# A fused attention and MLP kernel: P V of the fourth batch as float32r products in parts, a rank for attention units, and the order of the tails' transfers

## The chip, the cores and the metric

One NeuronCore of a Trainium2 chip runs the whole program. The metric is device time in microseconds (us) of one execution; lower is better. The engines are named as the profile names them: PE is TensorE (PEld its weight loads), DVE is VectorE, ACT is ScalarE, POOL is GpSimd, SP the engine on whose queue most transfers are issued.

## The reference

Attention with rotary embedding over 4 batches, 8 heads, 576 positions and 64 columns a head; then two MLPs over the 512 columns of x, all in float32:

```
attn = softmax(rot(q) rot(k)^T / sqrt(64)) v          # 4 x 8 x 576 x 64
x  = attn, heads side by side                          # 4 x 576 x 512
xn = (x - mean) / sqrt(var + 1e-6) * g_ln
x  = x + relu(xn w_ch1) w_ch2                          # 512 -> 2048 -> 512
h  = gelu(x w_in);  u, v = halves of h                 # 512 -> 2 x 512
v  = (v - mean) / sqrt(var + 1e-6) * g2_ln
v  = w_sg v + b_sg                                     # over positions, 576 x 576
out = x + (u * v) w_out
```

## The kernel before

Activations lie transposed: columns on the partitions, positions along the free axis, in halves of HQ = 288. A large product is made of three float32r passes: both operands are split into a rounded high part and the rest, and high x high, low x high and high x low are summed in PSUM. The rounding is a copy on ACT, the rest a subtraction on DVE.

**Attention** (class Attn) runs in 64 units: four batches (groups 0 to 3), each eight blocks (a head pair p and a half hi), each block two heads j. A unit (`unit`, lines 302 to 366) does ten passes of scores (line 311: five key chunks, K and X each holding high and low part), a maximum over chunks (DVE, 334), a maximum over partitions (POOL, 337), then either adds the negative maximum on PE (`add`, 392) and takes the exponential (395), or subtracts it on DVE into sT (`subtract`, 376) and takes it there (381). The second form runs once all first-MLP weights are converted, so in most of batches three and four. Then P V (line 350): five products, one per key chunk, with sT and v as plain float32. The trace shows each as two passes, 640 in 64 units. Two ACT copies (357, 360) move the result and the row sums; the sums go by a transfer (364) to where the normalisation reads them. S is one tile, so a unit's scores wait until the one before has been subtracted; sT has two buffers (SB), K has four (KB).

**The first MLP** works on a batch at a time: `ln` and `rest` centre and split x (477 to 563; 512 the centred x, 524 and 528 its high and low part), `up` (655 to 657, relu parts 663 and 665) and `down` (685 to 687, ends 699 or 702, and in the last pass 708, 710 and the store 713). It runs on PE between the attention's steps of a later batch. Weights come in double precision and are converted while batch one and two are at work (lines 47 to 55, 635, 637). x0 has 17 tiles, so attention runs two batches ahead at most: two units of batch four run at 431 and 438 us, the other fourteen from 498 us on.

**The order** of all engines up to the end of the first MLP is written by a planner in the kernel, `Sched`: each step is a generator's yield of (engine, earliest start, cost, rank). It takes the step that can start first; a step of lower rank on the same engine that could start within HOLD = 0.4 of the chosen step's cost goes ahead of it. Ranks: relu and down ends 1, `ln` and `rest` 2, k, q and v preparation 3 to 3.2, weight loads 3.5, conversions 4, the second MLP's first loads 4.5, MLP products 5. A unit has rank 0 up to P V, which has 0.5. Engines keep that order on the chip.

**The second MLP** (`moe2`) begins as such a task when the last `up` pass has finished its first half (line 775 counts): `load_x(0)` issues eight transfers of x (937) and splits its four column slices on ACT (949) and DVE (951), the last two of them after `through()`, the end of the last up product. Then `load_tails(0)` issues four transfers (977) of the last 64 positions of batches one and two and splits them (ACT 981, DVE 983). The rest of `moe2` is ordered by the compiler's scheduler behind and between the planned steps: v in five chunks of positions (1006 to 1008, the fifth from the tails), each with its gelu (919 to 922) and statistics (1012, 1013), u (1038 to 1040), the root (1014, 1015), the normalisation and split of v (1019, 1023, 1025), the product over positions (1054 to 1058), and the output (963 to 967).

Of the kernel before, what the change touches and what calls it, by code (L numbers as in the profile page):

```python
# [14 lines left out]

NC5 = 5
HQ = 288
SB, QB, KB, AB = 2, 3, 4, 1
WB, WX, CB = 8, 3, 4
KC = (0, 256, 576)  # L20
KEY0 = (0, 128, 256, 384, 448)
L_CONV = 10.0
HOLD = 0.4
FG = [4, 8, 8, 4]

AHEAD = 2
# [6 lines left out]
def f32(ap):  # L33
    return ap.bitcast(F32)
# [90 lines left out]
def latest(*xs):  # L125

    return None if any(x is None for x in xs) else max(xs)


class Attn:  # L130
# [10 lines left out]
    def __init__(self, tc, ctx, k, groups, sched):  # L141
        self.tc, self.nc, self.k, self.groups, self.c = tc, tc.nc, k, groups, sched
        self.p = ctx.enter_context(tc.tile_pool(name="attn", bufs=2, side="right"))
        self.ps = ctx.enter_context(tc.tile_pool(name="attn_ps", bufs=1, space=PS))
        self.S = self.ps.tile([128, NC5, 512], F32, tag="S", name="S")
        self.Sfree = [0.0, 0.0]
        self.PV, self.X, self.qin, self.kin, self.vfree, self.sT = Bank(), Bank(2), Bank(QB), Bank(2), Bank(2), Bank(SB)
        self.K = Bank(KB)
        self.vin = [self.p.tile([128, NC5, 192], F32, tag=f"vin{i}", name=f"vin{i}", bufs=1) for i in range(2)]
        self.sums = [self.p.tile([64, HQ], F32, tag=f"sums{i}", name=f"sums{i}", bufs=1) for i in range(3)]  # L150
        self.last = {}
        self.done = []
        self.blocks, self.units = [], []
        for g, (b, halves) in enumerate(groups):
            if g == 0:
                order = [(hi, p) for hi in range(2) for p in range(4)]
            else:
                order = [(hi, p) for p in range(4) for hi in range(2)]
            for n, (hi, p) in enumerate(order):
                B = dict(g=g, b=b, hi=hi, h=halves[hi], p=p, n=len(self.blocks), left=2, k0=None, k=None, q=[None, None], v=None)  # L160
                self.blocks.append(B)
                B["newk"] = hi == 0
                B["newv"] = g == 0 or hi == 0
# [39 lines left out]
        return e  # L203

    def new_K(self, B):
        B["kslot"] = self.K.take()
        B["K"] = [self.p.tile([128, 576], F32R, tag=f"K{j}", name=f"K{j}", bufs=KB) for j in range(2)]

    def first(self):

# [36 lines left out]
    def prep(self, bi):  # L247

        nc, c, B = self.nc, self.c, self.blocks[bi]

        def k_task():
            e = yield "SP", self.kin.free, 0.7
            slot = self.kin.take()
            kin = self.p.tile([128, 2, 576], F32, tag="kin", name="kin")
            nc.sync.dma_start(out=kin, in_=self.k["k"][B["b"], B["p"]])
            yield "DVE", lambda: latest(e + 7.5, self.K.free()), 0.0
            self.new_K(B)
            e = yield from self.turn_k(kin, B["K"], 0, 576, 0.0)
            B["k0"] = B["k"] = e + 0.1
            self.kin.give(slot, e)  # L260

        def q_task():
            e = yield "SP", self.qin.free, 0.6
            slot = self.qin.take()
            qin = self.p.tile([128, 2, HQ], F32R, tag="qin", name="qin", bufs=QB)
            nc.sync.dma_start(out=f32(qin), in_=self.k["q"][B["b"], B["p"]][:, :, HQ * B["h"]:HQ * B["h"] + HQ])
            e = yield from self.rope(f32(qin), HQ, HQ * B["h"], e + (5.0 if bi == 1 else 7.0))
            e = yield from self.split(f32(qin[:, 0, :]), qin, e)
# [12 lines left out]

        if B["newk"]:
            c.task(k_task(), 3)
        c.task(q_task(), 3.1)

    def load_v(self, bi):
        nc, B = self.nc, self.blocks[bi]

        def v_task():
            e = yield "SP", self.vfree.free, 0.7  # L290
            slot = B["vslot"] = self.vfree.take()
            t = B["vin"] = self.vin[slot]
            for j in range(2):
                if j:
                    e = yield "SP", 0.0, 0.7
                nc.sync.dma_start(out=t[:, :, 128 * j:128 * j + 64], in_=self.k["v"][B["b"], B["p"]][:, :, j, :])
            B["v"] = e + 5.5

        if B["newv"]:
            self.c.task(v_task(), 3.2)  # L300


    def unit(self, i):
# [20 lines left out]
        if B["left"] == 0:  # L324
            self.X.give(B["xslot"], e + 0.1)
        Kb["kusers"] -= 1
        if Kb["kusers"] == 0:
            self.K.give(Kb["kslot"], e + 0.1)
        if i + 1 < len(self.units):
            c.task(self.unit(i + 1), 0)  # L330
        self.ahead(i)
        e = yield "DVE", e + 0.35, 1.68
        mx = self.p.tile([128, HQ], F32, tag="mx", name="mx", bufs=1)
# [6 lines left out]
        else:  # L340
            x1, slot, sT = yield from self.add(am, e)
        V = B["vof"]
        ps = None
        for c0, c1 in ((0, 2), (2, 5)):
            e = yield "PE", (lambda: latest(x1, self.PV.free(), V["v"])) if c0 == 0 else 0.0, 0.51 * (c1 - c0), 0.5
            if c0 == 0:
                bank = self.PV.take()
                ps = self.ps.tile([128, 512], F32, tag="PV", name="PV")[:, 0:HQ]
            for ch in range(c0, c1):
                nc.tensor.matmul(ps, V["vin"][:, ch, 64 * j:64 * j + 128], sT[:, ch, :], start=ch == 0, stop=ch == 4)  # L350
        self.sT.give(slot, e)
        V["users"] -= 1
        if V["users"] == 0:
            self.vfree.give(V["vslot"], e)
        a, b = 64 * j, 64 - 64 * j
        yield "ACT", e + 0.35, 0.41
        nc.scalar.copy(self.k["x0"](g, p, hi)[a:a + 64], ps[a:a + 64])  # L357
# [6 lines left out]
        nc.sync.dma_start(out=self.sums[self.sums_of(g, hi)][r:r + 1], in_=t[b:b + 1])  # L364
        if u["ends"]:
            self.done.append(e + 3.0)

    def new_sT(self):
        return self.sT.take(), self.p.tile([128, NC5, HQ], F32, tag="sT", name="sT", bufs=SB)
# [54 lines left out]
def fused_kernel(ctx, tc, q, k, v, cs, cst, w12, wi, wo, wsg, wsg4, gb, out):  # L424
# [35 lines left out]
        return x0_rel.get(x0_order[len(x0_order) - 17])  # L460

    attn_ctx = ExitStack()
    attn = Attn(tc, attn_ctx, dict(q=q, k=k, v=v, cs=csb, e=e128, x0=get_x0, x0_free=x0_free, spare=lambda: stored[0] == 32), groups, C)
    cctx = ExitStack()
    cpool = cctx.enter_context(tc.tile_pool(name="conv", bufs=1, side="right"))

# [285 lines left out]
    def mlp(parts):  # L752
        for d, g, F, i, hh in parts:
            n = FG[g]
            if g not in left:
                yield "PE", lambda: 0.0 if g != 1 or stored[0] == 32 else None, 0.0
                left[g] = 8
                if g == 1:
                    cctx.close()
                open_h(g)  # L760
                if g == NG - 1:
                    last_group()
            steps = down(g, F, i, hh) if d else up(g, n * F + i, hh)
# [135 lines left out]
def moe2(tc, M, hp, wpool, pp, B, x1d, w, gbt, eps, out, through):  # L899
# [23 lines left out]

    X = {}

    def load_x(b):
        if b >= B:
            return
        x1, at = {}, {}
# [9 lines left out]
        for c in range(4):  # L939
            if c == 2:  # L940
                yield "SP", lambda: 0.0 if through() else None, 0.0
            if c % 2 == 0:
                xh.append(M.tile([128, 2, 576], F32R, tag="xh", name="xh", bufs=2))
                xl.append(M.tile([128, 2, 576], F32R, tag="xl", name="xl", bufs=2))
# [27 lines left out]
    def load_tails(b):  # L972

        s = M.tile([128, 512], F32, tag="sq", name="tails", bufs=2)
        for c in range(4):
            e = yield "SP", 0.0, 0.6
            nc.sync.dma_start(out=s[:, 128 * c:128 * c + 128].rearrange("p (b q) -> p b q", b=2),
                              in_=x1d[b:b + 2, c, :, 512:576].rearrange("b p q -> p b q"))
        e = yield "ACT", (e or 0.0) + 4.0, 0.63
        tails[b] = t = M.tile([128, 2, 512], F32R, tag="w", name="w", bufs=WB)  # L980
        nc.scalar.copy(t[:, 0, :], s)
# [1 line left out]
        nc.vector.tensor_tensor(t[:, 1, :], s, f32(t[:, 0, :]), ALU.subtract)  # L983

    def at_once(steps):
        for _ in steps:
            pass

    yield from load_x(0)
    yield from load_tails(0)  # L990
    yield None
    for b in range(B):
        x1, xh, xl = X[b]
# [49 lines left out]
            final(b - 1)  # L1043
        at_once(load_x(b + 1))
        if b % 2 and b + 1 < B:
            at_once(load_tails(b + 1))
        gt = {}
        for hh in range(2):
            qs = slice(HQ * hh, HQ * hh + HQ)
# [79 lines left out]
```

## Time and profile before

| | us |
|---|---|
| median of 3 runs | 999.93 (998.19 to 1001.24) |
| profiled execution | 1002.52 |
| its span on the core | 1000.7 |
| PE busy | 939.7 |
| DVE busy | 714.2 |
| ACT busy | 444.6 |
| POOL busy | 91.4 |

The span runs from the first to the last instruction of the program; the execution's own time has 1.8 us around it. Busy times are of one execution, and engines overlap: 939.7 us of PE leave 61 us of the span in which it did nothing. PE's busy time counts a pass from its issue to its modelled end, so the distance between starts, not the duration, is what a pass costs in a row of passes. A groups row gives how many instructions of one line and shape there were, their busy time, the mean of one, and the idle time before them with what ended it.

### The profile page before, as it was taken

The numbers are of one execution on the slowest core, as the hardware profiler recorded it, in microseconds if no ns is written. First come the engines' busy times: TensorE is split into PE (matmuls) and PEld (weight loads), VectorE is DVE, ScalarE is ACT, GpSimd is POOL, SyncE is SP. The second block draws the span as 40 slices with busy tenths as digits, with TensorE's granted clock in tenths as the row PEclk, the third lists the DMA queues.
The fourth block names the chain that finished last, engine by engine and source line by source line (L and its number), as shares of the span: only waits on it lengthen the run. The fifth ranks groups of instructions, "written<-read, shape, count | busy, mean of one in ns | idle before, by whom it ended". The sixth has DMA issues, their size and how long they took to land.

```text
span 1000.7 us, 15881 instructions
## 1 busy us (share of the span) xinstructions
PE 939.7 (94%) x6057; PEld 867.8 (87%) x6057; DVE 714.2 (71%) x1188; ACT 444.6 (44%) x901; POOL 91.4 (9%) x78
## 2 busy tenths in 40 slices
PE   4688899999998889999999999999999979999998
PEld 3566688798898778989998999999999969989998
DVE  6998666699788788865589744586553887667764
ACT  3564554665434355443235531425222546345441
POOL 1121112122000211100012110000000000000000
PEclk9899999999999899999999999999999989999999
DMA  9888444378464564653755533588763300303011
GB/s 273 240 283 263 110 106 109 104 202 258 152 207 146 189 213 134 204 163 121 251 182 145 156 128 127 192 285 273 250 204 91 90 1 12 95 2 89 1 49 48
DMA packets 93420, 153.76 MB, mean 154 GB/s; under 512 B 38048, under 2 KB 60576, under 8 KB 93344
## 3 DMA queue, kind: packets, MB, share of 16 engines
q1 hardware_dynamic: 92800, 152.16, 49.1%
q8 instruction: 48, 0.79, 0.3%
q10 hardware_dynamic: 544, 0.59, 0.2%
q14 instruction: 28, 0.23, 0.1%
HBM read 107.25 MB, written 26.21 MB: 133 GB/s over the span
## 4 chain that ended last, share of the span: by engine, by line
PE 73%; DVE 14%; DMA 5%; ACT 2%; issue 2%; POOL 2%; SPq 1%; DVEq 0%; ACTq 0%; POOLq 0%
PE PV L350 8%; PE S L311 7%; PE m L686 6%; PE m L685 6%; PE m L687 6%; PE m L655 5%; PE m L657 5%; PE m L656 5%; DVE mx L334 4%; DMA sums<-sr 3%; PE S L392 2%; PE p L1054 2%; PE p L1055 2%; PE p L1056 2%; DVE sT L376 2%
## 5 line engine op out<-in xcount | busy, mean ns | idle before, releaser
L350 PE MATMUL PV<-sT,vin 128*128 128x288 f32 x640 | 170.8, 413 | 3.6 <-ACT sr L360 1.8
L655 PE MATMUL m<-xh,w 128*128 128x288 f32 x480 | 148.0, 308 | 2.4 <-DVE h L665 2.3
L350 PEld LDWEIGHTS PV<-sT,vin 128*128 128x128 f32 x640 | 120.1, 194 | 32.7 <-ACT sr L360 2.7
L685 PE MATMUL m<-h,w 128*128 128x288 f32 x480 | 145.2, 302 | 0.0
L686 PE MATMUL m<-h,w 128*128 128x288 f32 x480 | 142.0, 296 | 0.0
L334 DVE TENSOR_REDUCE mx<-S 128x288 f32<-128x1440 f32 x64 | 106.0, 1657 | 49.9 <-PE S L311 48.8
L656 PE MATMUL m<-xl,w 128*128 128x288 f32 x480 | 141.5, 295 | 0.0
L657 PE MATMUL m<-xh,w 128*128 128x288 f32 x480 | 141.2, 294 | 0.0
L687 PE MATMUL m<-h,w 128*128 128x288 f32 x480 | 140.5, 293 | 0.0
L337 POOL PARTITION_ALL_REDUCE am<-mx x64 | 89.3, 1395 | 500.4 <-DVE mx L334 500.4
L311 PE MATMUL S<-X,K 128*128 128x288 f32 x640 | 112.6, 321 | 16.8 <-ACT X L200 10.2
L311 PEld LDWEIGHTS S<-X,K 128*128 128x128 f32 x640 | 95.5, 201 | 29.2 <-ACT sT L395 11.0
L665 DVE SCALAR_TENSOR_TENSOR h<-m,h 128x288 fp32r<-128x288 f32 x128 | 58.0, 454 | 66.6 <-ACT h L663 65.8
L655 PEld LDWEIGHTS m<-xh,w 128*128 128x128 f32 x480 | 90.0, 188 | 6.5 <-DVE h L665 3.6
L663 ACT ACTIVATE h<-m 128x288 fp32r<-128x288 f32 x128 | 52.2, 408 | 95.0 <-PE m L657 94.5
L656 PEld LDWEIGHTS m<-xl,w 128*128 128x128 f32 x480 | 90.2, 188 | 1.4
L686 PEld LDWEIGHTS m<-h,w 128*128 128x128 f32 x480 | 90.2, 188 | 1.0
L685 PEld LDWEIGHTS m<-h,w 128*128 128x128 f32 x480 | 90.0, 188 | 1.1
L657 PEld LDWEIGHTS m<-xh,w 128*128 128x128 f32 x480 | 90.3, 188 | 0.0
L687 PEld LDWEIGHTS m<-h,w 128*128 128x128 f32 x480 | 90.2, 188 | 0.0
L357 ACT COPY x<-PV 64x288 f32<-64x288 f32 x64 | 25.2, 394 | 137.8 <-PE PV L350 137.7
L395 ACT ACTIVATE sT<-S 128x576 f32<-128x576 f32 x74 | 53.6, 769 | 29.7 <-PE S L392 28.3
(149 smaller groups left out, 1848.9 us busy)
## 6 DMA issues: line engine op xcount, KB each, us to landing
w<-wsc SPq DMA_DIRECT2D x96, 512.0 KB, 4.3
X<-qin SPq DMA_DIRECT2D x124, 144.0 KB, 2.6
cd<-in_w SPq DMA_DIRECT2D x32, 512.0 KB, 6.1
wsc<-w SPq DMA_DIRECT2D x24, 512.0 KB, 3.6
qin<-in_q SPq DMA_DIRECT2D x31, 288.0 KB, 4.4
kin<-in_k SPq DMA_DIRECT2D x15, 576.0 KB, 5.0
vin<-in_v SPq DMA_DIRECT2D x40, 160.0 KB, 4.2
x1d<-x SPq DMA_DIRECT2D x32, 144.0 KB, 2.7
```

Of the source, the lines that this page charges most:

```text
L311: x = nc.tensor.matmul(S[:, ch, 0:HQ], Kb["K"][j][:, KEY0[ch]:KEY0[ch] + 128], B["X"][:, j, 1 - t, :], start=t == 0, stop=t == 1)
L334: nc.vector.tensor_reduce(mx, S[:, :, 0:HQ].rearrange("p c q -> p q c"), AX.X, ALU.max)
L337: nc.gpsimd.partition_all_reduce(am, mx, 128, bass_isa.ReduceOp.max)
L350: nc.tensor.matmul(ps, V["vin"][:, ch, 64 * j:64 * j + 128], sT[:, ch, :], start=ch == 0, stop=ch == 4)
L395: ex.append(nc.scalar.activation(sT[:, c0:c1, :], self.S[:, c0:c1, 0:HQ], AF.Exp, scale=0.125))
L655: nc.tensor.matmul(ps, w[:, 0, ms], xh[:, kc, :], start=kc == 0, stop=False)
L656: nc.tensor.matmul(ps, w[:, 0, ms], xl[:, kc, :], start=False, stop=False)
L657: nc.tensor.matmul(ps, w[:, 1, ms], xh[:, kc, :], start=False, stop=kc == 3)
L665: nc.vector.scalar_tensor_tensor(t[:, 1, :], ps, 0.0, f32(t[:, 0, :]), op0=ALU.max, op1=ALU.subtract)
L685: nc.tensor.matmul(ps, w[:, 0, ms], t[:, 0, :], start=a == 0, stop=False)
L686: nc.tensor.matmul(ps, w[:, 1, ms], t[:, 0, :], start=False, stop=False)
L687: nc.tensor.matmul(ps, w[:, 0, ms], t[:, 1, :], start=False, stop=a == n - 1)
```

## The change

In batch four, P and v are split. `load_v` makes vh (ACT copy) and vl (DVE subtraction) of a pair's v, 960 columns each; `split_P` makes Ph and Pl of a unit's sT in two pieces of 576 and 864 columns. P V is then fifteen float32r passes: vh Ph, vl Ph and vh Pl for each key chunk. vh, vl, Ph and Pl have one buffer each, in a pool that opens with the first MLP's second batch. A step of no length on PE waits until v's time is known.

A unit of batches two to four has rank 2.5 up to P V (UNIT), where it had 0. K has three buffers; the tile of batch one's fourth pair lies in the conversion pool. In `moe2` the tails' four transfers are issued before those of x, and their split (`split_tails`) stands behind `through()`, ahead of the third slice of x.

```diff
-SB, QB, KB, AB = 2, 3, 4, 1
+SB, QB, KB, AB = 2, 3, 3, 1
+UNIT = (0, 2.5, 2.5, 2.5)
...
-            B["v"] = e + 5.5
+            e += 5.5
+            if self.p2 and B["g"] == 3:
+                e = yield "ACT", lambda: latest(e, self.V2.free()), 1.1
+                B["v2"] = self.V2.take()
+                B["vh"], B["vl"] = (self.p2.tile([128, NC5, 192], F32R, tag=x, name=x) for x in ("vh", "vl"))
+                nc.scalar.copy(B["vh"], t)
+                e = yield "DVE", e + 0.1, 1.15
+                nc.vector.tensor_tensor(B["vl"], t, f32(B["vh"]), ALU.subtract)
+            B["v"] = e + 0.1
...
-            c.task(self.unit(i + 1), 0)
+            c.task(self.unit(i + 1), UNIT[self.units[i + 1]["g"]])
...
+        if self.p2:
+            yield "PE", lambda: V.get("v"), 0.0
+        if "vh" in V:
+            P, x1 = yield from self.split_P(sT, slot, x1)
...
-                nc.tensor.matmul(ps, V["vin"][:, ch, 64 * j:64 * j + 128], sT[:, ch, :], start=ch == 0, stop=ch == 4)
-        self.sT.give(slot, e)
+                terms = (("vh", P[0]), ("vl", P[0]), ("vh", P[1])) if P else (("vin", sT),)
+                for n, (v, x) in enumerate(terms):
+                    nc.tensor.matmul(ps, V[v][:, ch, 64 * j:64 * j + 128], x[:, ch, :], start=ch == n == 0,
+                                     stop=ch == 4 and n == len(terms) - 1)
...
+    def split_P(self, sT, slot, at):
+        nc, e = self.nc, [at, 0.0]
+        for i, (c0, c1) in enumerate(((0, 2), (2, 5))):
+            e[i] = yield "ACT", (lambda: latest(at, self.P2.free())) if i == 0 else 0.0, 0.1 + 0.29 * (c1 - c0)
+            if i == 0:
+                self.P2.take()
+                P = [self.p2.tile([128, NC5, HQ], F32R, tag=x, name=x) for x in ("Ph", "Pl")]
+            nc.scalar.copy(P[0][:, c0:c1, :], sT[:, c0:c1, :])
+        for i, (c0, c1) in enumerate(((0, 2), (2, 5))):
+            x = yield "DVE", e[i] + 0.1, 0.1 + 0.32 * (c1 - c0)
+            nc.vector.tensor_tensor(P[1][:, c0:c1, :], sT[:, c0:c1, :], f32(P[0][:, c0:c1, :]), ALU.subtract)
+        self.sT.give(slot, x)
+        return P, x + 0.1
...
-    def load_x(b):
+    def load_x(b, between=()):
...
             if c == 2:
                 yield "SP", lambda: 0.0 if through() else None, 0.0
+                yield from between
...
-    yield from load_x(0)
-    yield from load_tails(0)
+    s = yield from load_tails(0)
+    yield from load_x(0, split_tails(0, *s))
```

## Rows read from the trace of the kernel before

**Rows 1.** The page's busy table: us (share), instructions.

```profile
PE 939.7 (94%) x6057; PEld 867.8 (87%) x6057; DVE 714.2 (71%) x1188; ACT 444.6 (44%) x901; POOL 91.4 (9%) x78
```

**Rows 2.** Stretches: us; PE, PEld, DVE, ACT, POOL busy (instructions); PEclk, DMA share, GB/s.

```profile
327.50:332.80 5.30, 5.28 (x18) 4.65 (x19) 4.10 (x8) 3.03 (x6) 0.00 (x0) 0.50 0.02 4
498.00:600.00 102.00, 101.50 (x635) 91.72 (x634) 75.89 (x83) 46.77 (x88) 17.22 (x14) 1.00 0.52 155
600.00:672.00 72.00, 71.33 (x534) 70.87 (x534) 42.53 (x90) 19.56 (x46) 0.00 (x0) 1.00 0.59 197
771.00:803.00 32.00, 32.00 (x216) 30.18 (x214) 24.38 (x58) 15.04 (x34) 0.00 (x0) 1.00 0.25 75
803.00:810.20 7.20, 0.01 (x1) 0.00 (x0) 6.76 (x18) 5.93 (x15) 0.00 (x0) 0.80 0.00 0
810.24:814.10 3.86, 3.86 (x14) 3.54 (x15) 3.83 (x8) 2.65 (x5) 0.00 (x0) 0.50 0.01 2
```

**Rows 3.** DVE's and PE's timelines at the dip near 325 us.

```profile
324.33 1.65 DVE L334 TENSOR_REDUCE mx<-S 128x288 f32<-128x1440 f32 x1
325.90 2.21 DVE L528 SCALAR_TENSOR_TENSOR xl<-xc,gbt,xh 128x288 fp32r<-128x288 f32 x4
...
327.48 1.57 PE L392 MATMUL S<-am,e 128*128 128x288 f32 x5 [4.18 <-POOL am L337]
```

**Rows 4.** ACT's, DVE's and PE's timelines up to 810 us.

```profile
770.86 0.62 ACT L981 CAST w<-tails 128x512 fp32r<-128x512 f32 x1
...
795.37 0.45 DVE L710 TENSOR_TENSOR x<-acc,x 128x288 f32<-128x288 f32 x1
795.74 0.69 DVE L983 TENSOR_TENSOR w<-tails,w 128x512 fp32r<-128x512 f32 x1
...
799.44 0.39 PE L1008 MATMUL p<-wih,w 128*128 128x512 f32 x1
...
810.24 1.09 PE L1054 MATMUL p<-wgh,w 128*128 128x288 f32 x3 [7.24 <-ACT w L1023]
```

**Rows 5.** PE's timeline near 510 us (start, us); line 350's durations.

```profile
509.12 1.49 PE L311 MATMUL S<-X,K 128*128 128x288 f32 x10
511.24 2.59 PE L350 MATMUL PV<-sT,vin 128*128 128x288 f32 x10
...
L350 PE MATMUL PV<-sT,vin x640: 403/406/687, 21.5 to 598.7; 128*128 128x288 f32 x160
```

**Rows 6.** DVE's and PE's timelines after the fourth batch's attention.

```profile
613.67 1.54 DVE L512 TENSOR_TENSOR xc<-x,ln 128x288 f32<-128x288 f32 x4 [1.12 <-PE ln L508]
...
671.94 0.29 PE L655 MATMUL m<-xh,w 128*128 128x288 f32 x1
```

**Rows 7.** Groups by line and shape: busy us, mean ns, idle before.

```profile
L376 DVE TENSOR_TENSOR sT<-S,am 128x1440 f32<-128x1440 f32 x27 | 44.6, 1650 | 9.2 <-POOL am L337 9.0
L892 DVE TENSOR_TENSOR wgl<-st,wgh 128x576 fp32r<-128x576 f32 x5 | 3.8, 755 | 0.3
L890 ACT CAST wgh<-st 128x576 fp32r<-128x576 f32 x5 | 3.3, 668 | 0.0
L395 ACT ACTIVATE sT<-S 128x864 f32<-128x864 f32 x37 | 32.8, 887 | 0.3
```

**Rows 8.** POOL's timeline, fourth batch.

```profile
548.93 2.11 POOL L337 PARTITION_ALL_REDUCE am<-mx  x1 [5.20 <-DVE mx L334]
...
584.41 1.15 POOL L337 PARTITION_ALL_REDUCE am<-mx  x1 [5.79 <-DVE mx L334]
591.34 1.15 POOL L337 PARTITION_ALL_REDUCE am<-mx  x1 [5.77 <-DVE mx L334]
```

**Rows 9.** DVE's timeline beside the first of these.

```profile
548.68 1.35 DVE L176 TENSOR_TENSOR kin<-kin,csb 128x1152 f32<-128x1152 f32 x1
```

**Rows 10.** SP queue's timeline at the start of the second MLP.

```profile
751.20 3.75 SPq L937 DMA_DIRECT2D x<-x1d  x8
755.00 1.97 SPq L977 DMA_DIRECT2D tails<-x1d  x4
```

More of the change, by code (lines that the diff above doesn't have):

```diff
@@ L150, in __init__ @@
         self.sums = [self.p.tile([64, HQ], F32, tag=f"sums{i}", name=f"sums{i}", bufs=1) for i in range(3)]
+        self.p2, self.ctx = None, ctx
+        self.P2, self.V2 = Bank(), Bank()
         self.last = {}
@@ L205, in new_K @@
     def new_K(self, B):
-        B["kslot"] = self.K.take()
-        B["K"] = [self.p.tile([128, 576], F32R, tag=f"K{j}", name=f"K{j}", bufs=KB) for j in range(2)]
+        last = (B["g"], B["p"]) == (0, 3)
+        B["kslot"] = None if last else self.K.take()
+        B["K"] = [(self.k["pool"]() if last else self.p).tile([128, 576], F32R, tag=f"K{j}", name=f"K{j}", bufs=1 if last else KB)
+                  for j in range(2)]
     def first(self):
@@ L255, in k_task @@
             nc.sync.dma_start(out=kin, in_=self.k["k"][B["b"], B["p"]])
-            yield "DVE", lambda: latest(e + 7.5, self.K.free()), 0.0
+            yield "DVE", lambda: latest(e + 7.5, self.K.free() if (B["g"], B["p"]) != (0, 3) else 0.0), 0.0
             self.new_K(B)
@@ L326, in unit @@
         Kb["kusers"] -= 1
-        if Kb["kusers"] == 0:
+        if Kb["kusers"] == 0 and Kb["kslot"] is not None:
             self.K.give(Kb["kslot"], e + 0.1)
         if i + 1 < len(self.units):
-            c.task(self.unit(i + 1), 0)
+            c.task(self.unit(i + 1), UNIT[self.units[i + 1]["g"]])
         self.ahead(i)
@@ L342, in unit @@
         V = B["vof"]
-        ps = None
+        ps = P = None
+        if self.p2:
+            yield "PE", lambda: V.get("v"), 0.0
+        if "vh" in V:
+            P, x1 = yield from self.split_P(sT, slot, x1)
         for c0, c1 in ((0, 2), (2, 5)):
-            e = yield "PE", (lambda: latest(x1, self.PV.free(), V["v"])) if c0 == 0 else 0.0, 0.51 * (c1 - c0), 0.5
+            e = yield "PE", (lambda: latest(x1, self.PV.free(), V["v"])) if c0 == 0 else 0.0, (0.41 if P else 0.51) * (c1 - c0), 0.5
             if c0 == 0:
@@ L349, in unit @@
             for ch in range(c0, c1):
-                nc.tensor.matmul(ps, V["vin"][:, ch, 64 * j:64 * j + 128], sT[:, ch, :], start=ch == 0, stop=ch == 4)
-        self.sT.give(slot, e)
+                terms = (("vh", P[0]), ("vl", P[0]), ("vh", P[1])) if P else (("vin", sT),)
+                for n, (v, x) in enumerate(terms):
+                    nc.tensor.matmul(ps, V[v][:, ch, 64 * j:64 * j + 128], x[:, ch, :], start=ch == n == 0,
+                                     stop=ch == 4 and n == len(terms) - 1)
+        if P:
+            self.P2.give(0, e)
+        else:
+            self.sT.give(slot, e)
         V["users"] -= 1
@@ L354, in unit @@
             self.vfree.give(V["vslot"], e)
+            if P:
+                self.V2.give(V["v2"], e)
         a, b = 64 * j, 64 - 64 * j
@@ L366, in unit, with open_split @@
             self.done.append(e + 3.0)
+    def open_split(self):
+        self.p2 = self.ctx.enter_context(self.tc.tile_pool(name="attn2", bufs=1, side="right"))
+    def split_P(self, sT, slot, at):
[11 more added lines that the diff above has]
+        return P, x + 0.1
     def new_sT(self):
@@ L462, in fused_kernel @@
     attn_ctx = ExitStack()
-    attn = Attn(tc, attn_ctx, dict(q=q, k=k, v=v, cs=csb, e=e128, x0=get_x0, x0_free=x0_free, spare=lambda: stored[0] == 32), groups, C)
+    attn = Attn(tc, attn_ctx, dict(q=q, k=k, v=v, cs=csb, e=e128, x0=get_x0, x0_free=x0_free, spare=lambda: stored[0] == 32, pool=lambda: cpool), groups, C)
     cctx = ExitStack()
@@ L760, in mlp @@
                 open_h(g)
+                if g == 1:
+                    attn.open_split()
                 if g == NG - 1:
@@ L974, in load_tails @@
         s = M.tile([128, 512], F32, tag="sq", name="tails", bufs=2)
+        e = None
         for c in range(4):
@@ L978, in load_tails, with split_tails @@
                               in_=x1d[b:b + 2, c, :, 512:576].rearrange("b p q -> p b q"))
+        return s, e
+    def split_tails(b, s, e):
         e = yield "ACT", (e or 0.0) + 4.0, 0.63
@@ L985, in at_once @@
     def at_once(steps):
-        for _ in steps:
-            pass
-    yield from load_x(0)
-    yield from load_tails(0)
+        while True:
+            try:
+                next(steps)
+            except StopIteration as x:
+                return x.value
+    s = yield from load_tails(0)
+    yield from load_x(0, split_tails(0, *s))
     yield None
@@ L1045, in moe2 @@
         if b % 2 and b + 1 < B:
-            at_once(load_tails(b + 1))
+            at_once(split_tails(b + 1, *at_once(load_tails(b + 1))))
         gt = {}
```

## The prediction

> **What bounds the kernel now.** I read the busy table first: TensorE (PE) is busy 94% of the span [rows 1]. The slices of the page put most of the rest into the first eighth, and single dips near 325 and 810 us. Then the stretches by window: from 498 to 600 us, where the fourth batch's attention runs between products of the MLP, PE is busy 101.5 of 102 us, and from 600 to 672 us 71.3 of 72 [rows 2]. So there the number of PE passes sets the time, and VectorE (75.9 and 42.5 us busy) and ScalarE are covered. Two places are set by a wait: PE idles 4.18 us before line 392 at 327.5 us, waiting for the partition maximum [rows 3], and 7.24 us before line 1054 at 810.2 us [rows 4]. [...]
>
> **P V of the fourth batch (16 units).** Now each unit is ten float32 passes. A block of ten starts at 511.24 and lasts 2.59 us; with 0.406 us for its last pass that is (2.59 - 0.406)/9 = 0.243 us a pass, two passes a key chunk: 0.485 us. The ten float32r passes of the scores beside it give (1.49 - 0.29)/9 = 0.133 us a pass [rows 5], the 0.29 being one such pass by itself [rows 6], and three of them replace the two: 0.398 us. All these new products have the shape of the scores' (128x128 weights, 288 columns), so I take that price. The saving is 0.087 us x 5 chunks x 16 units = 6.9 us, straight off a stretch in which PE is the bound.
>
> What pays for it: ScalarE rounds P in two pieces, 576 and 864 columns. The cast of 576 took 0.668 us, an Exp of 864 0.887 us [rows 7]: 1.56 us a unit. VectorE subtracts the same pieces: 0.755 us for 576 columns, and from the 1.65 us of 1440 columns the slope is 1.04 ns a column, so 1.05 us for 864 [rows 7]: 1.81 us a unit. v, 960 columns, costs by the same slopes about 1.0 us of ScalarE and 1.15 us of VectorE for each of four head pairs. Over 16 units VectorE gets 33.6 us and ScalarE 29 us. Only two units of the batch run ahead of 498 us; the other fourteen bring VectorE 25.3 + 3.5 = 28.8 us. Between 498 and 672 us VectorE has (102 - 75.9) + (72 - 42.5) = 55.6 us free [rows 2], so the work fits, but not inside the 102 us: VectorE would be full. Units now start 6.93 us apart (584.41 to 591.34) [rows 8]; I estimate 8 to 9 us with the split, since the single Ph/Pl buffer makes rounding, subtracting (1.56 + 1.81 us, partly side by side) and 2.0 us of products one loop, and VectorE owes each unit its maximum, its subtraction (1.65 us) and the split. The last P V then moves from 598.7 us [rows 5] to between 615 and 626. The split of a pair's first unit also waits for vh and vl, whose one buffer comes free with the last P V of the pair before: three turns of some 2.2 us (1.0 + 1.15), which that range holds; behind them on ScalarE and VectorE stand the next units' steps and the MLP's relu copies. What hides this is the MLP of batch three, which PE works on meanwhile.
>
> How far that cover reaches: the first half's centred x is there at 615.2 us (613.67 + 1.54) [rows 6], 16.5 us after the last pass of P V; rounding and subtracting it adds some 3 us, so the first half needs about 20 us after the last P V. The second half repeats the centring, and I allow it 32 us. The fourth MLP begins at 671.9 us [rows 6], 665 with PE's saving, its second half one pass of four weights (6.5 us) later. 671.5 - 32 is 639.5: the attention may end some 40 us later before PE waits; I use 15 to 27. I charge 1.0 us for PE stalls where its fixed order has a product ahead of a late Pl (in this stretch before, PE lost 0.5 us) [rows 2]; bounds 0 and 4.
>
> One row speaks of contention: a partition reduce took 2.11 us at 548.9 instead of 1.15 [rows 8], while VectorE ran a multiply of two SBUF operands, 548.68 to 550.03 [rows 9]. The new subtractions are of that kind. [...] By the row, up to 0.96 us comes on top of each unit: 14 x 0.96 = 13 us on the end of the attention, still within the 40.
>
> **The tails of the second MLP.** The fifth chunk of its v part needs both parts of the tails. ScalarE rounds them at 770.86, but VectorE subtracts only at 795.74, behind the last store-side addition of the fourth MLP (line 710, 795.37) [rows 4]. The order is the hand planner's, by its own costs: the subtraction (rank 4.5, 0.7 us) comes up among the down products, each of which owes VectorE 1.39 us in every 1.62; the 0.23 us left are under HOLD x 0.7 = 0.28, so it is put off until there are no more. The chunk's product with that part starts at 799.44 [rows 4], and from there the chain of gelu, statistics, root, normalisation and rounding runs, at its end with nothing on PE: 7.24 us. After that PE ran 810.24 to 814.10 at clock 0.50 [rows 2], which costs half of it, 1.9 us.
>
> In the changed order the tails' transfers go first, and the split stands between the second and third slice of x, at the end of the last up product, before the first down product owes VectorE anything. So it gets its place about 24 us earlier, the fifth chunk ends with the other four (near 780), and the products of u, which now run before it, cover the chain. Left in its place: VectorE, which was busy 24.4 us of the 32 between 771 and 803 and 6.8 of the 7.2 us after [rows 2], would have to do all of it, 31.1 us, in 32. I take 1.5 us of idle left (bounds 0 and 6). The four tails transfers pass eight x transfers on SP's queue: 1.97 us of issuing [rows 10], so x lands that much later; ScalarE's x copies stand in line before the relu copies of the last up products, whose PSUM banks wait for them. I charge 1.0 us (bounds 0 and 2). Sum: -7.2 - 1.9 + 1.5 + 1.0 = -6.6 us.
>
> **Rank 2.5 for units of batches two to four.** It moves the score, maximum and subtraction steps behind the ends (rank 1) and the normalisation (rank 2) in the planner's choice. Where PE is full it only shifts MLP against attention. At 323 us it may put line 528's four subtractions (2.21 us, at 325.90) ahead of the unit's maximum, which now precedes them [rows 3]: 2.2 us more idle, or, if the order there comes out well, the 4.18 us and half of 5.3 us at clock 0.50 [rows 2] are won. I take 0; bounds -6.8 and +4. **The K tile**: three buffers instead of four cover two pairs at work and one coming; the fourth pair of batch one lies in the conversion pool. Cost 0, hidden by the MLP; without that cover a unit would be late by at most one interval, 6.9 us.
>
> **Sum.** -6.9 + 1.0 - 6.6 + 0 = -12.5 us. The profiled execution took 1002.5 us (span 1000.7), 2.6 above the median of the runs, 999.93. 990.0 there, 987.4 at the median: I say 987.5.
>
> **Rivals.** (1) Tails not cured: VectorE's queue still holds the split, or x's third and fourth slice, behind the down ends; then the 9.1 us stay and only P V is won: 987.5 + 6.6 = 994. For it: the x slices behind the split will have to fit between the 1.39 us blocks. Against: the split is ahead of them. (2) The rank closes the dip at 327 us as well: 987.5 - 6.8 = 981. (3) New waits in PE's fixed order eat the gains (the planner reorders three batches): 10 us of them give 998, no change. (4) Slower: VectorE-bound attention of batch four outlasts its cover. It decides at a last P V of about 639 us; each us beyond is one of PE idle ahead of the fourth MLP, and half a clock behind it. Units 12 us apart (14 x 12 + 498 = 666) give 27 us of idle and some 3 of clock: 1017. Against it: VectorE owes a unit about 8 us. (5) The products don't get cheaper: if three passes took 0.485 us too, 994; the scores' rows speak against it.
>
> **Chances.** The contention row is why rival 4 gets 0.06 and not less. Forecast 0.55; rival 1 0.16, rival 2 0.12, rival 3 0.08, rival 4 0.06, rival 5 0.03. A measurement tells about 0.3%, 3 us, from no change. Faster by more: 0.55 + 0.16 + 0.12 + 0.03 = 0.86, less 0.02 for a poor sum of bounds: 0.84; within: 0.09; slower: 0.07. The range takes in rivals 1, 2 and 5 with their spread: 979 to 997.
>
> **What would show it.** PE's group of P V in the last batch: 240 passes at 0.133 us where 160 at 0.243 stood; last P V at 610 to 630 us with PE full; the first fourth-batch up product near 665; line 983's successor near 771 and no idle above 2 us before line 1054's; clock 1.00 there. Wrong would be idle PE in the last batch's attention, idle before the fourth MLP, or third x slices behind the last line 710.

## The result, and the profile after

| | before | after |
|---|---|---|
| median of 4 runs, us | 1000.46 (998.19 to 1001.24) | 988.65 (986.94 to 991.42) |
| profiled execution / its span, us | 1002.52 / 1000.7 | 989.17 / 987.4 |

The ratio is 0.9888, 95% interval 0.986 to 0.9917: 11.8 us faster, where 12.5 were forecast. The sum came out, but its terms did not: the one set to zero earned most, and the one for the tails failed in just this combination. First the busy table of the page, against [rows 1]:

```profile
PE 926.0 (94%) x6107; PEld 865.3 (88%) x6107; DVE 756.5 (77%) x1230; ACT 472.2 (48%) x937; POOL 90.0 (9%) x78
```

PE is busy 13.7 us less with 50 passes more. The split adds 80 (240 for 160); the other 30 went elsewhere, see below. The span is 13.3 us shorter: in total PE idles as long as before, but not in the same places. Stretches of the kernel after (columns as in [rows 2]):

```profile
498.00:600.00 102.00, 100.64 (x744) 98.28 (x743) 87.83 (x96) 62.42 (x113) 17.22 (x12) 1.00 0.52 155
600.00:648.00 48.00, 47.50 (x354) 46.84 (x353) 32.67 (x71) 15.63 (x35) 0.00 (x0) 1.00 0.59 189
787.20:795.58 8.38, 0.00 (x1) 0.00 (x1) 6.50 (x18) 7.34 (x17) 0.00 (x0) 0.78 0.00 0
795.58:802.10 6.52, 6.52 (x26) 6.21 (x27) 4.90 (x9) 2.65 (x5) 0.00 (x0) 0.50 0.01 3
```

In the 102 us from 498 us on, PE idles 1.4 us, where it idled 0.5 before [rows 2]; 1.0 was charged. The stall before the product over positions is still there, 8.4 us, with 6.5 us at clock 0.50 behind it: the passes of that product start 0.24 us apart there (797.76 to 801.84), and 0.133 right after at clock 1.00 (802.24 to 804.91). PE's timeline (start, us; in brackets the idle before and its releaser) shows the dip that had stood at 327 us [rows 3], first and last pass of one P V block of fifteen, the start of the fourth MLP, and the last stages [rows 4]:

```profile
322.76 0.40 PE L535 MATMUL ln<-rc,sel 128*128 128x288 f32 x1 [3.00 <-DVE x L537]
...
601.32 0.30 PE L369 MATMUL PV<-Ph,vh 128*128 128x288 f32 x1
...
603.18 0.29 PE L369 MATMUL PV<-Pl,vh 128*128 128x288 f32 x1
...
648.05 0.30 PE L698 MATMUL m<-xh,w 128*128 128x288 f32 x1
...
763.64 0.50 PE L1061 MATMUL p<-wih,w 128*128 128x512 f32 x1 [2.14 <-DVE w L1033]
...
774.21 0.40 PE L1091 MATMUL p<-xh,wih 128*128 128x288 f32 x1 [2.18 <-ACT sq L964]
...
795.58 1.81 PE L1107 MATMUL p<-wgh,w 128*128 128x288 f32 x6 [8.42 <-ACT w L1076]
```

The fourth MLP starts at 648.0, 23.9 us earlier than [rows 6]; the product over positions at 795.6, only 14.7 earlier. Nine us were given back in between. The line that names the cause is the first of the last three: PE waits for L1033, VectorE's subtraction of the tails. VectorE's timeline there (L708 relu, L937 weight conversions of the second MLP, L997 the slices of x, L753 the last step of a down end), and two casts on ScalarE's:

```profile
736.33 0.46 DVE L997 TENSOR_TENSOR xl<-x,xh 128x288 fp32r<-128x288 f32 x1 [0.41 <-ACT xh L995]
...
741.74 0.46 DVE L708 SCALAR_TENSOR_TENSOR h<-m,h 128x288 fp32r<-128x288 f32 x1 [0.63 <-ACT h L706]
742.25 0.69 DVE L937 TENSOR_TENSOR wol<-ce,woh 128x512 fp32r<-128x512 f32 x1
743.81 0.46 DVE L745 TENSOR_TENSOR acc<-m,acc 128x288 f32<-128x288 f32 x1 [0.87 <-PE m L730]
...
750.90 0.45 DVE L997 TENSOR_TENSOR xl<-x,xh 128x288 fp32r<-128x288 f32 x1
...
754.97 0.45 DVE L997 TENSOR_TENSOR xl<-x,xh 128x288 fp32r<-128x288 f32 x1
...
762.52 0.46 DVE L753 TENSOR_TENSOR x<-acc,x 128x288 f32<-128x288 f32 x1
762.90 0.68 DVE L1033 TENSOR_TENSOR w<-tails,w 128x512 fp32r<-128x512 f32 x1
763.50 1.56 DVE L997 TENSOR_TENSOR xl<-x,xh 128x288 fp32r<-128x288 f32 x4
```

```profile
742.78 0.62 ACT L1031 CAST w<-tails 128x512 fp32r<-128x512 f32 x1
743.30 1.44 ACT L995 CAST xh<-x 128x288 fp32r<-128x288 f32 x4
```

ScalarE had rounded the tails by 743.4 and the last slices of x by 744.7. VectorE subtracts them some 19 us later, behind the last down end (762.52). Four of the eight x subtractions now stand there as well, which in the kernel before was the place of the tails alone [rows 4].

### The profile page after: what moved, and what is told of

Read it like the earlier page. It is cut to its first block, busy times and chain, and to the rows that moved or that the text cites. A ratio compares the mean times of both kernels' runs of the same rounds, so it can differ in the third digit from the quotient of the medians.

```text
span 987.4 us, 16043 instructions
## 1 busy us (share of the span) xinstructions
PE 926.0 (94%) x6107; PEld 865.3 (88%) x6107; DVE 756.5 (77%) x1230; ACT 472.2 (48%) x937; POOL 90.0 (9%) x78
## 4 chain that ended last, share of the span: by engine, by line
PE 83%; DVE 8%; ACT 3%; DMA 3%; issue 2%; POOL 1%; SPq 1%; DVEq 0%; ACTq 0%
PE PV L369 12%; PE S L324 8%; PE m L698 7%; PE m L700 6%; PE m L699 6%; PE m L728 6%; PE m L729 6%; PE m L730 6%; PE p L1107 2%; DVE mx L347 2%; PE p L1108 2%; PE p L1109 2%; PE p L1010 2%; PE p L1009 2%; PE S L435 2%; PE p L1011 2%
## 5 line engine op out<-in xcount | busy, mean ns | idle before, releaser
L369 PE MATMUL PV<-sT,vin 128*128 128x288 f32 x480 | 126.0, 409 | 1.3 <-ACT sr L385 0.9
L369 PEld LDWEIGHTS PV<-sT,vin 128*128 128x128 f32 x480 | 89.0, 192 | 22.4 <-ACT sr L385 1.4
L708 DVE SCALAR_TENSOR_TENSOR h<-m,h 128x288 fp32r<-128x288 f32 x128 | 57.7, 452 | 44.3 <-ACT h L706 43.8
L424 ACT ACTIVATE sT<-sT 128x576 f32<-128x576 f32 x66 | 51.0, 800 | 32.8 <-DVE sT L419 32.7
```

The source lines that it names most:

```text
L369: nc.tensor.matmul(ps, V[v][:, ch, 64 * j:64 * j + 128], x[:, ch, :], start=ch == n == 0, stop=ch == 4 and n == len(terms) - 1)
L708: nc.vector.scalar_tensor_tensor(t[:, 1, :], ps, 0.0, f32(t[:, 0, :]), op0=ALU.max, op1=ALU.subtract)
```

## The experiments

Three parts, each with and without the others, make eight kernels; the kernel before and after are two of them. The moved K tile is in e1, e4, e6 and e12, and not in e2 and e3. All medians are of at least four runs; ratios are to runs of the kernel before made beside them (its medians there: 1000.0 to 1000.9).

| rank 2.5 | tails first | split | | median, us | ratio, 95% interval |
|---|---|---|---|---|---|
| x | | | e3 | 982.36 | 0.983 (0.9804 to 0.9856) |
| | x | | e2 | 991.0 | 0.9914 (0.9888 to 0.994) |
| | | x | e4 | 999.86 | 0.9998 (0.9983 to 1.0014) |
| x | x | | e6 | 973.0 | 0.9732 (0.9708 to 0.9757) |
| x | | x | e1 | 977.79 | 0.9782 (0.9756 to 0.9808) |
| | x | x | e12 | 991.78 | 0.9912 (0.9892 to 0.9933) |
| x | x | x | after | 988.65 | 0.9888 (0.986 to 0.9917) |

**The parts one at a time, and the old order of the tails (e1 to e4).** In e1 the changed kernel gets the order of the kernel before:

```diff
+    yield from load_x(0)
     s = yield from load_tails(0)
-    yield from load_x(0, split_tails(0, *s))
+    yield from split_tails(0, *s)
```

so that the tails' transfers stand behind those of x again, too.

> The changed kernel, with the tails' transfers and split put back behind the slices of x. Theory A: in the changed kernel the two x slices that all of v and u need stand behind the down ends in VectorE's order, and that costs about 9 us between the first up product of batch four and line 1107's first (147.6 us there, 138.3 before); with the old order they stand ahead of the down ends again, and the dip of before (7 to 9 us, for the late tails) stays: 979 to 981 us. Rival: the order of the tails makes no difference, and the dips are there because PE comes to this place 24 us earlier than VectorE's conversions are done: 988 to 989 us.

Measured 977.79, a little below what theory A gave: the new order costs the changed kernel 10.9 us. The dip of before doesn't stay as it was: PE waits 5.04 us for the late tails at 770.60, before the fifth chunk's products, and not before the product over positions. Alone, in the kernel before, the new order does better. That is e2:

> The kernel before with the new order of the tails alone. Theory A: without the fourth batch's extra work the second MLP's weights are converted by 743 us, the x slices find VectorE free, the tails' split stands ahead of the down ends, and the step of the prediction holds: -6.6 us, 994 us, with less than 3 us idle ahead of the product over positions. Rival: the new order costs by itself (x lands 2 us later, and PE waits for it): 1002 us or more.

Measured 991.0, 9.4 us less than before (the interval allows 6 to 11), with no idle PE ahead of the product over positions. The step was right by itself.

In e3 the kernel before gets the rank alone, with `UNIT = (0, 2.5, 2.5, 2.5)` and

```diff
-            c.task(self.unit(i + 1), 0)
+            c.task(self.unit(i + 1), UNIT[self.units[i + 1]["g"]])
```

> The kernel before with rank 2.5 for the units of batches two to four alone. Theory A: the rank slows attention down and lets the weight conversions and the first batch's MLP through earlier, which is where 13 to 17 us came from ahead of the fourth MLP: 984 to 987 us, with the second MLP pass starting some 25 us earlier than 352.8. Rival (the prediction): it only shifts work, 998 to 1001 us, and the gain came from elsewhere (the K tile, the split).

Measured 982.36: the rank alone earns 18.1 us, more than even theory A gave. Where, is read from two groups of the kernel before, then the same of e3 (one line further down in its code): the additions of the negative maximum, and the subtractions that end the conversion of the first MLP's weights, with their first and last start:

```profile
L392 PE MATMUL S<-am,e 128*128 128x288 f32 x185 | 35.8, 327 | 22.7 <-POOL am L337 22.2
...
L637 DVE TENSOR_TENSOR wx<-ce,wx x8: 677/687/693, 77.1 to 338.1; 128x512 fp32r<-128x512 f32 x8
```

```profile
L393 PE MATMUL S<-am,e 128*128 128x288 f32 x155 | 29.1, 321 | 19.1 <-POOL am L338 19.1
...
L638 DVE TENSOR_TENSOR wx<-ce,wx x8: 681/688/1022, 74.8 to 271.6; 128x512 fp32r<-128x512 f32 x8
```

Units that yield to the MLP's ends and the layer norm come further apart (in the kernel after, partition reduces start at 203.03, 212.27 and 221.54, before at 200.48, 207.34 and 214.51), and the conversions end 66.5 us earlier. Units take the subtracting form once they have ended, so six more of them do, and 30 passes of `add` go: 30 x 0.133 = 4.0 us of PE. The rest is idle time. The stretches between the first up products of batches one, two and three, before and in e3:

```profile
124.30:352.80 228.50, 219.39 (x1381) 199.87 (x1381) 180.73 (x280) 116.53 (x226) 34.48 (x23) 0.99 0.54 166
352.80:525.20 172.40, 167.86 (x1107) 155.85 (x1106) 125.52 (x170) 71.67 (x146) 19.59 (x16) 1.00 0.58 178
```

```profile
120.40:322.10 201.70, 196.63 (x1281) 182.55 (x1280) 167.03 (x257) 106.31 (x203) 23.11 (x19) 1.00 0.59 191
322.10:499.60 177.50, 176.56 (x1147) 163.81 (x1147) 142.13 (x193) 80.27 (x161) 25.60 (x19) 0.99 0.55 166
```

PE idled 9.1 + 4.5 = 13.6 us in the two, and 5.1 + 0.9 = 6.0 with the rank: 7.6 us. With the 4.0 that is 11.6. The two profiled spans differ by 20.7 us. Of these, 3.9 stand ahead of the first stretch (124.30 and 120.40), and 3.9 already at the last addition of batch one that PE waits for (107.51 before, 103.65 in e3, 105.82 in e4 with rank 0 throughout), so I don't count them as the rank's. About 1 us, by my estimate, is the clock: 5.3 us of work at 0.50 near 327 before [rows 2], with the rank 3.4 (in e3 passes start 0.24 us apart from 322.36 to 325.72; in the kernel after, 324.30 to 327.70 has clock 0.50). The other 4 us I did not follow.

The split alone is e4: the changed kernel with `UNIT = (0, 0, 0, 0)` and the old order of the tails.

> The changed kernel with rank 0 for all units and the old order of the tails: what is left is P V of batch four in parts and the K tile. Theory A: 80 x 0.087 = 6.9 us less PE work, the rest hidden: 993 to 994 us. Rival: VectorE's 33.6 us more make PE wait in its fixed order, or the later weights of the second MLP do: 997 to 1003 us.

Measured 999.86, the rival: the saved passes are paid back. No run has the K tile alone with rank 0, so its share in this is open. PE's stretch in e4, beside [rows 2], and one of its new waits:

```profile
498.00:600.00 102.00, 97.63 (x710) 94.86 (x710) 89.31 (x102) 59.96 (x105) 18.29 (x12) 0.98 0.54 163
...
521.09 0.70 PE L592 MATMUL ln<-lt,ones 128*64 128x288 f32 x2 [1.39 <-DVE h L708]
...
522.70:526.10 3.40, 3.40 (x13) 2.22 (x11) 2.43 (x5) 1.53 (x4) 0.00 (x0) 0.50 0.10 22
```

PE idles 4.4 us there instead of 0.5, and 3.4 us run at clock 0.50: passes of lines 699 and 700 start 0.24 us apart at 522.86, 0.13 at 526.85. I estimate half as lost, 1.7. That is 5.6 us, where the passes save 6.9.

**Why the tails fail (e6, e5, e8, e9, e12).** First whether the split has a hand in it: e6 is the changed kernel with float32 P V everywhere.

```diff
-            if self.p2 and B["g"] == 3:
+            if self.p2 and B["g"] == 4:
```

> The changed kernel without the split of P and v (float32 P V in all batches; rank, tails and K tile kept). Theory B: without the split's work the conversions are done in time, the tails' split stands ahead of the down ends, and rank and tails add up: 1000.4 - 18.1 - 9.4 = 973 us, faster than the changed kernel by 15 although PE has 6.9 us more to do. Rival: the tails' order fails here too, since the rank alone brings PE there 20 us earlier: 989 to 992 us.

Measured 973.0, as the rank and the tails sum to: 1000.4 - 18.1 - 9.4 = 972.9. That sum leaves nothing for the moved K tile, which e6 has and e2 and e3 have not. Next, the rank of the whole second-MLP task:

```diff
-    C.task(ahead(), 4.5)
+    C.task(ahead(), 3.9)
```

> The changed kernel with rank 3.9 instead of 4.5 for the second MLP's first loads and splits, so that they go ahead of the weight conversions (rank 4). Theory B: the tails' new order is good and fails in the changed kernel only because the split of P pushes the last conversions of the second MLP's weights into the same few us, where they hold the x slices back until the down ends fill VectorE: with the rank the tails' split stands ahead of the down ends, the three dips at 764 to 796 us go, and the time is that of the old tails (977.8) less about 8: 968 to 971 us. Rival: PE reaches this place too early for VectorE whatever the order: 978 to 988 us.

Measured 981.02, a miss for theory B. VectorE's timeline of e5 shows what is still late:

```profile
742.21 0.69 DVE L1033 TENSOR_TENSOR w<-tails,w 128x512 fp32r<-128x512 f32 x1
...
747.94 0.45 DVE L997 TENSOR_TENSOR xl<-x,xh 128x288 fp32r<-128x288 f32 x1
...
762.02 0.45 DVE L753 TENSOR_TENSOR x<-acc,x 128x288 f32<-128x288 f32 x1
762.39 0.45 DVE L997 TENSOR_TENSOR xl<-x,xh 128x288 fp32r<-128x288 f32 x1
```

The tails came early, but the last slices of x still trail between the down ends, whose rank of 1 is ahead of 3.9 as of 4.5: the last subtraction starts 15.8 us after the first down end (746.58), in e6 only 7.3 us after it (753.15 to 760.45). All chunks need these slices, and PE waits 8.15 us before line 1107. So early tails are not enough; this step brought 7.6 us. Rank 0 for batch four's units:

```diff
-UNIT = (0, 2.5, 2.5, 2.5)
+UNIT = (0, 2.5, 2.5, 0)
```

> The changed kernel with rank 0 for the units of batch four. Theory D: with rank 0 the split earns nothing (new PE waits on VectorE of 6.5 us, as in the split alone), while the tails' split keeps its place ahead of the down ends: 971 to 974 us, the time of rank and tails alone. Rival: the split's loss in the split-alone run came from batches two and three, and here its 6.9 us show: 965 to 967 us.

Measured 969.6 (ratio 0.9696, 0.9674 to 0.9718), below what theory D gave and above the rival. The tails keep their place, as theory D said; that the split earns nothing here is not borne out (e11 below). VectorE in e8, then its last weight conversion and first down end in e6:

```profile
735.49 0.69 DVE L937 TENSOR_TENSOR wol<-ce,woh 128x512 fp32r<-128x512 f32 x1
...
736.95 1.19 DVE L997 TENSOR_TENSOR xl<-x,xh 128x288 fp32r<-128x288 f32 x3
...
742.15 0.69 DVE L1033 TENSOR_TENSOR w<-tails,w 128x512 fp32r<-128x512 f32 x1
...
747.42 0.46 DVE L745 TENSOR_TENSOR acc<-m,acc 128x288 f32<-128x288 f32 x1 [2.03 <-PE m L730]
```

```profile
725.05 0.68 DVE L937 TENSOR_TENSOR wol<-ce,woh 128x512 fp32r<-128x512 f32 x1
...
753.15 0.46 DVE L745 TENSOR_TENSOR acc<-m,acc 128x288 f32<-128x288 f32 x1 [2.38 <-PE m L730]
```

From the last weight conversion (735.49 + 0.69) to the first down end VectorE has 11.2 us for x and the tails, in e6 27.4 (725.05 + 0.68 to 753.15). In the changed kernel it has 743.81 - 742.94 = 0.9. Both ends of the slot moved: the loads of these weights begin when batch four's layer norm is through, at 622.53 in e6 and, behind the longer attention with the split (last P V at 608.4 instead of 586.1), at 643.78 in the changed kernel, while the first down end comes 9.3 us earlier. I read this as the lost slot: what stands in line no longer fits before the ends take over. A lost slot alone isn't enough, though. In e1, with the old order, the last conversion (748.32 + 0.69) even ends after the first down end has started (748.93), and e1 takes 977.79. If it is the new order in a slot too small, giving only the slices and the tails a rank ahead of the ends must do as well, with batch four untouched. That is e9, in `load_x` and `split_tails` (a step without a rank of its own keeps the last one, so VectorE's steps follow ScalarE's):

```diff
-                e = yield "ACT", at[c, hh] + 4.0, 0.42
+                e = yield "ACT", at[c, hh] + 4.0, 0.42, 0.9
...
-        e = yield "ACT", (e or 0.0) + 4.0, 0.63
+        e = yield "ACT", (e or 0.0) + 4.0, 0.63, 0.9
```

> The changed kernel (988.65 us), with the ScalarE and VectorE steps that split the slices of x and the tails for the second MLP set to rank 0.9, just below the 1 of the relu and down ends, where they had the task's 4.5. Nothing else is changed. Theory E (what the combination lost is one queue: VectorE's planned order puts the third and fourth slice of x and the tails' subtraction behind the last down end): with the rank they come ahead of the down ends, the fifth chunk of v runs with the others, and the 2.1, 2.2 and 8.4 us of idle PE before the last stage are gone, with most of the half clock behind them: 968 to 972 us, the last stages as long as in the kernel with the tails alone. Rival (the order is not the cause; VectorE has too much left at the end, so that the down ends, now later, hold the last MLP's PSUM banks and PE waits there instead): 978 to 988 us, with idle PE ahead of the last down products.

Measured 970.1 (0.9706, 0.967 to 0.9741), as theory E gave: 18.6 us from the place of these ScalarE and VectorE steps alone. PE in e9 from the last up products to the product over positions, and VectorE's lines:

```profile
727.00:780.00 53.00, 53.00 (x356) 50.28 (x356) 40.07 (x89) 26.50 (x56) 0.00 (x0) 1.00 0.33 101
...
741.49 0.69 DVE L1033 TENSOR_TENSOR w<-tails,w 128x512 fp32r<-128x512 f32 x1
...
745.71 1.20 DVE L997 TENSOR_TENSOR xl<-x,xh 128x288 fp32r<-128x288 f32 x3 [0.17 <-ACT xh L995]
...
747.19 0.45 DVE L745 TENSOR_TENSOR acc<-m,acc 128x288 f32<-128x288 f32 x1
...
783.18 0.68 DVE L937 TENSOR_TENSOR wol<-ce,woh 128x512 fp32r<-128x512 f32 x1
```

PE has no idle time in 53 us. What gives way is the last weight conversion: it stands at 783.18 instead of 742.25, behind the down ends, and PE doesn't wait for it. Last, the prediction's own premise, the split and the tails with the rank left out:

```diff
-UNIT = (0, 2.5, 2.5, 2.5)
+UNIT = (0, 0, 0, 0)
```

> The changed kernel with all ranks of units back at 0, so the split and the new order of the tails without the rank: this is the sum of the prediction with its rank term left out, which it set to 0. Theory H (the prediction's two terms hold side by side, P V -5.9 and tails -6.6): 987 to 989 us. Theory I (they add as each did alone: split 0, tails -9.4): 990 to 992 us. Rival (the tails fail with the split whatever the rank, as in the changed kernel, where x's third and fourth slice came behind the down ends): 999 to 1004 us, with some 12 us of idle PE before the product over positions.

Measured 991.78: theory I. With units at rank 0 the tails earn 8.1 us beside the split (e4 to e12), close to their 9.4 alone, and the split still earns nothing.

**Where the rank acts (e7).** Rank 2.5 for batch two only, in the kernel before (with the task line of e3):

```diff
+UNIT = (0, 2.5, 0, 0)
```

> The kernel before with rank 2.5 for the units of batch two alone. Theory C: what the rank buys is the earlier end of the first MLP's weight conversions (271.6 instead of 338.1 us), which run beside batch two; so most of the 18.1 us comes from batch two: 984 to 988 us. Rival: every batch gives its part: 992 to 995 us.

Measured 993.94 (0.9936, 0.9916 to 0.9956), the rival. The conversions end as early as in e3 and the 30 passes are gone, but the dip stays:

```profile
326.86 2.77 PE L312 MATMUL S<-X,K 128*128 128x288 f32 x10 [5.03 <-DVE sT L377]
```

So early conversions don't shorten the dip. With the rank in batch three as well it is shorter, but not gone: 2.99 us in e3, 3.00 before line 535 in the kernel after and in e8, where batch four has rank 0. By medians batch two brings 6.5 us of the 18.1, and batch four 4.4 (e11 below, without the split and with rank 0 in batch four, took 977.36, e6 973.0); that leaves some 7 for batch three, if the parts add.

**What the split earns (e10, e11).** In e10 the split alone goes without Pl.

```diff
-                P = [self.p2.tile([128, NC5, HQ], F32R, tag=x, name=x) for x in ("Ph", "Pl")]
+                P = [self.p2.tile([128, NC5, HQ], F32R, tag=x, name=x) for x in ("Ph",)]
...
-        for i, (c0, c1) in enumerate(((0, 2), (2, 5))):
-            x = yield "DVE", e[i] + 0.1, 0.1 + 0.32 * (c1 - c0)
-            nc.vector.tensor_tensor(P[1][:, c0:c1, :], sT[:, c0:c1, :], f32(P[0][:, c0:c1, :]), ALU.subtract)
-        self.sT.give(slot, x)
-        return P, x + 0.1
+        self.sT.give(slot, e[1])
+        return [P[0], P[0]], e[1] + 0.1
```

> The split alone (ranks 0, old order of the tails: 999.86 us), leaving out Pl: VectorE's subtraction of the rounded P is not made, and the third product of each key chunk uses Ph once more, so the low part of P is missing from the result. PE's passes, ScalarE's rounding and the single buffer of Ph stay. Theory F (the 6.9 us that the passes save were paid back because VectorE is full, 16 x 1.8 = 29 us more): without the subtraction the idle PE and the half clock of the third batch's first up products (10.0 us over full-clock passes, 3.5 before) shrink to 3 to 5, and the time is 993 to 995 us. Rival (the wait comes with the split whatever VectorE owes: ScalarE's rounding, the single buffer, or where the planner places the layer norm of batch three): 997 to 1000 us.

Measured 999.15 (0.9982, 0.9963 to 1.0): the rival. The stretch of e10, and one of its waits:

```profile
498.00:600.00 102.00, 98.58 (x728) 96.15 (x727) 72.45 (x82) 59.85 (x105) 16.02 (x12) 1.00 0.56 169
...
524.57 0.70 PE L589 MATMUL ln<-lt,ones 128*64 128x288 f32 x2 [0.79 <-ACT rstd L596]
```

VectorE is down from 89.3 to 72.5 us of 102, less than before the change, and PE still idles 3.4 us. A full VectorE is not what eats the split alone. e11 is e8 without the split:

> The best kernel so far (rank 2.5 in batches two and three only, split, new order of the tails: 969.6 us) without the split: float32 P V in all four batches, 160 passes of 0.243 us where 240 of 0.133 us stand. It stands to that one as the kernel with rank 2.5 in all three batches and no split (973.0) stands to the changed kernel (988.65). Theory G (with batch four's rank at 0 the split earns what its passes save): 976 to 977 us. Rival (the split earns about half of it there, 3.4 us, the rest of the 969.6 being no more than the tails and the rank): 972 to 974 us. Second rival (batch four's rank, not the split, is what the tails needed, and the split earns nothing): 969 to 971 us.

Measured 977.36 (0.9781, 0.9743 to 0.9819) against e8's 969.6: theory G. There the split earns 7.8 us, with intervals of some 2 to 4 us on either side; with rank 2.5 in all three batches 4.6 beside the old tails (e3 to e1) and 2.9 beside the new in order (e6 to e9); with all ranks 0 nothing (e4, and e2 to e12). So rank 0 in batch four is not what costs the split its gain: in e8 batch four has rank 0, and the gain is there. It is lost where batches two and three have rank 0 as well, as e8's rival supposed; the moved K tile, which e4 and e12 have and the kernels that they are compared with have not, may have a part in it.

## Why the prediction was right or wrong

**P V.** The price was right: fifteen passes start within 603.18 - 601.32 us, 14 steps of 0.133, as [rows 5] gave for the scores. What was mis-sized is the charge "1.0 us for PE stalls where its fixed order has a product ahead of a late Pl": in the change it was about that, for the split alone 5.6 to 6.3, above the bound of 4 (idle 3.9 more in 498 to 600, 0.7 more after, 1.7 for the clock of 0.50). For the split alone rival 3 came true. And the waits weren't on Pl: the largest of e4 from 498 us on are 1.39 and 0.93 us on the relu part (line 708) and 0.93 on a transfer into X. Which step of the planner puts PE's products ahead of these stays open; e10 only excludes the 29 us of VectorE that the subtractions of P take, and e8 against e11 says that it goes with rank 0 in batches two and three (or with the K tile at that rank).

**The attention's end.** Batch four's last fourteen units came 8.7 us apart on average ((594.01 - 481.15)/13, by their partition reduces), as estimated, with intervals from 7.2 to 15.6. But with the rank they begin at 481 us and not at 498, so the last P V stood at 608.4, ahead of the 615 to 626 forecast. Rival 4 was never near.

**Contention.** Part of POOL's and VectorE's timeline after:

```profile
481.15 1.15 POOL L350 PARTITION_ALL_REDUCE am<-mx  x1 [39.73 <-DVE mx L347]
...
562.55 1.51 POOL L350 PARTITION_ALL_REDUCE am<-mx  x1 [7.88 <-DVE mx L347]
...
584.31 1.97 POOL L350 PARTITION_ALL_REDUCE am<-mx  x1 [5.74 <-DVE mx L347]
594.01 1.16 POOL L350 PARTITION_ALL_REDUCE am<-mx  x1 [7.73 <-DVE mx L347]
...
562.30 2.19 DVE L407 TENSOR_TENSOR Pl<-sT,Ph 128x576 fp32r<-128x576 f32 x2
```

Three reduces in a row took 1.51 us beside such a pair, and one 1.97 beside the subtraction of v. The twelve that begin between 498 and 600 us took 17.22 us, 1.44 each; but the fourteen of before took 17.22 in that window too [rows 2], 1.23 each. So with the split a reduce is 0.2 us longer on average, not the 0.96 that I carried as a bound. Beside the pair it is 0.36 us longer than the 1.15 of 481.15, and the pair takes 2.19 us where two pairs with no reduce beside them took 1.72 (at 542.11 and 555.49). At 553.5 us it is the subtraction of v that is longer, 1.62 instead of 1.15 (519.31), and the reduce takes 1.21. What makes them longer no run shows.

**The tails.** Alone, the step held, and by the median better than forecast: 9.4 us where 6.6 stood, as if the 9.1 us were won whole and the charges of 1.5 and 1.0 for crowded ends and late x copies cost nothing. In the change it failed, and the failing sentence is "So it gets its place about 24 us earlier". That place exists only while VectorE has time between the last weight conversion and the first down end. I placed it in the order of the kernel before, and not in the one that the rank and the split make. Rival 1 named the mechanism ("VectorE's queue still holds the split, or x's third and fourth slice, behind the down ends"), and its price too was short: it leaves the 9.1 us as before, where the runs show 10.9 more than with the old order; half of x is late as well, and with the tails early but x late e5 won back 7.6 us of the 18.6 of e9.

**The rank.** "Where PE is full it only shifts MLP against attention. [...] I take 0" is the step that failed most: -18.1 us, far outside -6.8 to +4. It looked at one place, the dip, and even there rival 2 was too high: the dip isn't closed but shortened, from 4.18 us of idle and 5.3 of work at clock 0.50 to 2.99 and 3.4, which is some 2 us and not 6.8. What it left out is what the units' VectorE steps had kept waiting: the conversions, and through them the form that later units take (30 passes), and the waits between the first up products of batches one and three (13.6 to 6.0 us).

**The sum.** Parts alone: -18.1 - 9.4 - 0.6 = -28.1, which would be 972. Any two of them add up to within 4 us (e6 0.1 off, e12 1.4, e1 3.9 better). All three together lose 16. That 988.65 came so near the forecast of 987.5 is luck: a gain that the sum had set to 0 and a loss that it had only as a rival cancel. e9 shows 970 for the same parts with the steps in another order, and e8 the same without batch four's rank.

## What to carry to other kernels

A step that is placed by ranks has its place only in the order that all parts of a change make together: work out which engine's free slot it uses, and whether another part of the same change fills or moves that slot. A rank is not free where an engine is full; ask which later work it lets through, and what changes form once that work is done. And when a measured total agrees with a sum, run the parts one by one before believing the terms.
